# Linear attention and a gated feed-forward layer: keys of the third batch in the first chunk, two accumulators in turn, and turned queries and rows loaded at once

## The chip, the cores and the metric

The kernel runs on one core of a Trainium2 chip. The core has five engines that run side by side, each with its own queue of instructions: TensorE (PE in the profile; its weight loads are PEld), VectorE (DVE), ScalarE (ACT), GpSimd (POOL) and SyncE (SP), which here issues all DMA transfers. The metric is the time of one execution on the device in microseconds; several timed runs are given with their median. A profile is one further execution, recorded instruction by instruction.

## The reference

There are 8 batches with 8 heads, 576 tokens a batch and 64 elements a head. Linear attention is followed by a gated feed-forward layer over all 4608 tokens:

```python
q_s = exp(q - max(q, axis=-1));  q_s = q_s / (sum(q_s, axis=-1) + 1e-9)   # per token and head
k_s = exp(k - max(k, axis=2));   k_s = k_s / (sum(k_s, axis=2) + 1e-9)    # over a batch's tokens
kv  = einsum('bhsd,bhse->bhde', k_s, v)                                   # 64 x 64 per head
x   = einsum('bhsd,bhde->bhse', q_s, kv)       # -> x of 4608 x 512
out = ((x @ w_a) * (x @ w_b)) @ w_out          # 512 -> 1536 -> 512
```

All inputs are float32.

## The kernel before

**Chunks.** The 4608 tokens are worked in nine chunks of 512 tokens. Each chunk needs `x` of its own tokens (attention) and then runs the feed-forward layer over them. Two heads make a group (`g`, four of them), so that a group fills 128 partitions. A batch has 576 tokens and a chunk 512, so a chunk needs the `kv` matrices of one or two batches. float32 products are made as three products of a high and a low part (`split`, L76: ScalarE or VectorE writes the high part, VectorE the low part as a difference).

**The first chunk** (L636 to L651) goes over 12 blocks `f` of the inner dimension. Each step loads the weights of a later block, converts them from the 64-bit form in which they arrive (`to_float`, L87: ScalarE, VectorE, GpSimd, VectorE), writes parts of them back to DRAM, multiplies (`gate_first`, L419) and projects the block before (`project_first`, L457). Beside this runs the attention of the second chunk.

**The chunks after it** (L666 to L729) make the gated products with seven block products instead of eight (`product`, L443), for six steps `i` of two blocks. The seven weight operands of a step come from DRAM (`get_w`, L163, eight buffers `ws`), or, in the second chunk, are partly formed from sums by GpSimd (`sums`, L168) and then split. The seven operands that stand for `x` are formed by `x_operands` (L392) from the tile `xf`, which the attention fills.

**Attention beside the products.** `attention_tasks(c)` (L490) returns a list of steps for chunk `c`, and each step is a list of functions. `Spread` (L571) hands these steps out, so many at each call: `attend()` once for each `f` from 1 in the first chunk, `attend(last)` three times for each `i` later. In the later chunks, VectorE's instructions of a call are queued behind the VectorE instruction `last` (`issue_after`); those of other engines aren't. Apart from that a planner orders each engine's instructions: it takes those that are ready by its own estimates, earlier ones of the program first. It also gives out buffers: tiles with one tag share a number of buffers (`bufs`), and a new tile waits until an older one of that tag has been read for the last time. PSUM has eight banks here, under the tags `at`, `k0`, `k1`, `k2` and `po0` to `po3`.

**Keys.** For each batch and group: load keys and values (`k_load`, `v_load`, two buffers each), maximum over the tokens, subtract, exponential (`kv_soft`, L198), product with the values (`kv_product`, L248), and split (`kv_split`, L267). For the third batch (`b == 2`) the maximum over the partitions goes over PE: a transpose `pm`, a reduction and a diagonal matrix on VectorE, and a product `pmx` (L206 to L216); for later batches it is one instruction of GpSimd. The loop of L494 adds a batch's keys to the tasks of the first chunk that needs it; for the third batch that is chunk 2, whose attention runs beside the products of chunk 1, the second chunk.

**Queries.** For the second chunk (`c < LATE`, which is 2) a group's queries are normalised as rows, turned by PE (`q_transpose`, L361: `pq`), split, and multiplied with `kv` (`x_product`, L372: `px`); ScalarE copies the result to `xf` (L532). Both `pq` and `px` have the tag `at`. For the chunks from the third on, rows give the statistics alone (`q_stats`, L317); these are turned and written to DRAM as `dq` (`q_stats_out`, L330). The queries are then read a second time in turned form from the input `qt_late` (tile `qtt`, tag `kt`, two buffers), and the statistics come back as rows repeated over 64 partitions (tile `mr`, two buffers; `q_turned`, L341). `q_exp` (L353) adds the negative maximum, takes the exponential and splits; after `px` VectorE multiplies by the reciprocal of the sum (L562). The three parts `b0` (loads), `b1` (`q_exp`) and `b2` (product) of the four groups are pipelined: in one step `b0` of a group, `b1` of the one before, `b2` of the one before that.

Of the kernel before, what the change touches and what calls it, by code (L numbers as in the profile page):

```python
# [29 lines left out]
def linear_attention_then_gated_ffn(  # L30
# [299 lines left out]
    def q_stats_out(c, st):  # L330

        n = NP * 2 * 2 * TT
        pst = ps.tile([n, P], F32, name="pst", tag="at")
        nc.tensor.transpose(pst, st.rearrange("p g h w j -> p (g h w j)"), ident)
        sst = sb.tile([n, P], F32, name="sst", bufs=1)
        nc.vector.tensor_copy(out=sst, in_=pst)
        dq = dr.tile([n, P], F32, name=f"dq{c}")
        nc.sync.dma_start(out=dq, in_=sst)
        return dq.rearrange("(g h wj) p -> g h (wj p)", g=NP, h=2)

    def q_turned(c, g, dq):  # L341

        qt = sb.tile([P, T], F32, name="qtt", tag="kt")
        nc.sync.dma_start(out=qt, in_=qt_late[c - LATE, g])
        mr = sb.tile([P, 2, T], F32, name="mr", bufs=2)
        for h in range(2):
            nc.sync.dma_start(
                out=mr[h * D:(h + 1) * D].rearrange("d w t -> d (w t)"),
                in_=dq[g, h].unsqueeze(0).broadcast_to([D, 2 * T]),
            )  # L350
        return qt, mr

    def q_exp(qt, mr):  # L353
        nc.vector.tensor_tensor(out=qt, in0=qt, in1=mr[:, 0], op=ALU.add)  # L354
        nc.scalar.activation(out=qt, in_=qt, func=AF.Exp)  # L355
        qh = sb.tile([P, T], F32R, name="qh", bufs=1)
        ql = sb.tile([P, T], F32R, name="ql", bufs=1)
        split(qh, ql, qt)
        return qh, ql
# [130 lines left out]
    def attention_tasks(c):  # L490

        xfs[c] = sb.tile([P, NP, T], F32, name="xf", bufs=1)
        steps = []
        for b in range(c * T // S, (c * T + T - 1) // S + 1):  # L494
            if b in batch_done:
                continue
            batch_done.add(b)
            for g in range(NP):
                box = {}

                def s0(b=b, g=g, box=box):
                    box["t"] = ((k_load_t if b == 1 else k_load)(b, g), v_load(b, g))

                def s1(b=b, box=box):
                    kt = box["t"][0]
                    box["e"] = kv_soft_t(kt, ("k2", "at")) if b == 1 else kv_soft(b, kt)

                def s2(b=b, g=g, box=box):
                    kv_split(b, g, kv_product(box["e"], box["t"][1]))

                steps.append((s0, s1, s2))
        def pipeline(steps):

            parts = max((len(p) for p in steps), default=0)
            return [
                [steps[i - j][j] for j in range(parts) if 0 <= i - j < len(steps)]
                for i in range(len(steps) + parts - 1)
            ]

        if c < LATE:  # L520
            for g in range(NP):
# [8 lines left out]
                def s2(c=c, g=g, box=box):  # L530
                    px = x_product(c, g, q_transpose(box["e"]))
# [4 lines left out]
        stats, last = [], []  # L536
        every = {}
        for g in range(NP):
# [15 lines left out]
            def b0(g=g, box=box):  # L554
                box["q"] = q_turned(c, g, every["dq"])

            def b1(box=box):
                box["e"] = q_exp(*box["q"])

            def b2(g=g, box=box):  # L560
                px = x_product(c, g, box["e"])
                nc.vector.tensor_tensor(out=xfs[c][:, g], in0=px, in1=box["q"][1][:, 1], op=ALU.mult)  # L562

            last.append((b0, b1, b2))
        stats, steps = pipeline(stats), pipeline(steps)
        seq = []
        for i in range(max(len(stats), len(steps))):
            seq.append((stats[i] if i < len(stats) else []) + (steps[i] if i < len(steps) else []))
        return seq + pipeline(last)
# [66 lines left out]
    for f in range(NF):  # L636
# [5 lines left out]
        if f:  # L642
            attend()
        if f == NF - 1:
# [138 lines left out]
```

## Time and profile before

| | |
|---|---|
| timed runs | 990.72, 988.35, 991.26 us; median 990.72 us |
| profiled execution | 984.57 us, its span 982.6 us |
| granted clock of TensorE, mean | 0.991 |
| DMA | 283.64 MB |

The page gives times in microseconds and calls engines by the short names above. "L449" is line 449 of the kernel before. In rows of groups stand, after the line, engine and operation, what is written and read ("out<-in"), the shape, the count ("x48"), then the busy time, the mean duration of one in ns, and the idle time of the engine just before them with what ended it. "PE px L381 <- DVE ql L82: 1.8, 3, 1.2" means that PE at L381 stood idle until VectorE's L82 was done, 1.8 us in all, three times, at most 1.2 us. In rows of a timeline stand start, duration, engine, line and operation, and in brackets the idle time before. PE's matmuls overlap, so their durations in a row add up to more than the time they take in sequence. In rows of windows the number in brackets is the count of instructions; the columns are named where the rows are shown.

### The profile page before, as it was taken

To read this page: it belongs to the slowest core of one execution; us is meant where nothing else is said; L and a number is where in the kernel's file an instruction comes from. 1 tells how busy PE (TensorE), PEld (TensorE's weight loads), DVE (VectorE), ACT (ScalarE), POOL (GpSimd) and SP (SyncE) were. 2 spreads that over 40 slices of the span, in tenths; PEclk is the share of its full clock that TensorE was granted. 3 is DMA by queue.
4 is the path that set the end of the run, shared out by engine and by line. 5 is a ranking of instruction groups with operands and counts; after the bars stand their busy time and mean duration, and the time that the engine had idled before them with its cause. 6 is when DMAs were issued, how large, how long until landed. Compare 5 with 4: busy or idle time off the path is not lost.

```text
span 982.6 us, 16989 instructions
## 1 busy us (share of the span) xinstructions
PE 948.5 (97%) x6171; PEld 851.9 (87%) x6171; DVE 629.2 (64%) x1257; ACT 391.4 (40%) x1085; POOL 112.8 (11%) x96
## 2 busy tenths in 40 slices
PE   4889999999999999999999999999999999999998
PEld 3657666899999999989999999999999999899997
DVE  7797786887685656656576557655666546653433
ACT  8665675632273325322442235223532263221101
POOL 3245345441000000000000000000000000000000
PEclk9799999999999999999999999999999999999999
DMA  9699858999989968997799779977998689767761
GB/s 347 222 412 402 343 207 294 373 327 305 301 285 352 320 237 280 325 328 250 248 335 324 271 251 345 319 270 257 331 299 299 220 300 283 274 224 271 246 207 61
DMA packets 93682, 283.64 MB, mean 289 GB/s; under 512 B 10848, under 2 KB 11424, under 8 KB 93600
## 3 DMA queue, kind: packets, MB, share of 16 engines
q1 hardware_dynamic: 93600, 282.57, 82.3%
q8 instruction: 49, 0.80, 0.3%
q14 instruction: 33, 0.27, 0.1%
HBM read 241.40 MB, written 37.98 MB: 284 GB/s over the span
## 4 chain that ended last, share of the span: by engine, by line
PE 78%; DMA 8%; DVE 5%; issue 4%; POOL 2%; ACT 2%; SPq 0%; POOLq 0%; DVEq 0%; ACTq 0%
PE po L470 25%; PE kp L449 13%; PE kx L449 13%; PE ka L449 12%; PE ky L449 6%; PE pk L251 3%; PE px L381 2%; POOL wr L103 2%; DMA mr<-dq 2%; PE po L459 2%; PE pt L426 2%; DMA qtt<-in_q_late 1%; DMA wo_raw<-in_w_out 1%; DMA dw<-ws 1%; DVE ws L82 1%
## 5 line engine op out<-in xcount | busy, mean ns | idle before, releaser
L470 PE MATMUL po<-wo_w,gh 128*128 128x512 f32 x768 | 227.2, 394 | 0.0
L449 PE MATMUL kx<-xo,ws 128*128 128x256 f32 x1152 | 164.5, 284 | 0.0
L449 PE MATMUL ka<-xo,ws 128*128 128x256 f32 x1152 | 162.3, 284 | 0.2
L470 PEld LDWEIGHTS po<-wo_w,gh 128*128 128x128 f32 x768 | 138.9, 189 | 26.2 <-ACT gh L79 0.3
L449 PE MATMUL kp<-xo,ws 128*128 128x256 f32 x1152 | 158.3, 284 | 0.8 <-DVE cc L712 0.8
L449 PEld LDWEIGHTS ka<-xo,ws 128*128 128x128 f32 x1152 | 151.2, 191 | 4.0 <-ACT xo L79 0.3
L449 PEld LDWEIGHTS kx<-xo,ws 128*128 128x128 f32 x1152 | 151.6, 191 | 3.4 <-issue 0.5
L449 PEld LDWEIGHTS kp<-xo,ws 128*128 128x128 f32 x1152 | 148.2, 191 | 3.6 <-DVE cc L712 1.0
L470 PE MATMUL po<-wo_w,gl 128*128 128x512 f32 x384 | 137.7, 396 | 0.0
L79 ACT CAST gh<-cc 128x512 fp32r<-128x512 f32 x96 | 57.7, 620 | 148.5 <-DVE cc L723 145.1
L722 DVE TENSOR_TENSOR cc<-kp,u 128x512 f32<-128x512 f32 x48 | 33.0, 688 | 89.2 <-PE kp L449 89.0
L323 ACT ACTIVATE qt<-qt,st 128x64 f32<-128x64 f32 x224 | 75.0, 337 | 31.7 <-DVE st L320 27.8
L470 PEld LDWEIGHTS po<-wo_w,gl 128*128 128x128 f32 x384 | 71.2, 188 | 15.8 <-DVE gl L82 0.4
L449 PE MATMUL ky<-xo,ws 128*128 128x256 f32 x576 | 79.4, 287 | 2.5 <-ACT xo L79 2.1
L426 PE MATMUL pt<-xo,ws 128*128 128x512 f32 x288 | 74.1, 406 | 4.0 <-ACT ga L433 3.2
L449 PEld LDWEIGHTS ky<-xo,ws 128*128 128x128 f32 x576 | 73.8, 194 | 3.2 <-ACT xo L79 2.4
L82 DVE TENSOR_TENSOR gl<-cc,gh 128x512 fp32r<-128x512 f32 x96 | 66.8, 703 | 9.4 <-ACT gh L79 9.2
L426 PEld LDWEIGHTS pt<-xo,ws 128*128 128x128 f32 x288 | 53.3, 188 | 20.4 <-ACT ga L433 4.7
L713 ACT COPY cc<-kx 128x256 f32<-128x256 f32 x48 | 17.8, 371 | 128.3 <-PE kx L449 120.6
L219 POOL PARTITION_ALL_REDUCE mx<-m x20 | 14.1, 704 | 470.9 <-DVE m L205 438.1
L712 DVE TENSOR_TENSOR cc<-kp,u 128x512 f32<-128x512 f32 x48 | 32.9, 684 | 52.3 <-PE kp L449 52.2
L355 ACT ACTIVATE qtt<-qtt 128x512 f32<-128x512 f32 x28 | 17.7, 633 | 107.4 <-DVE qtt L354 81.5
(126 smaller groups left out, 1238.7 us busy)
## 6 DMA issues: line engine op xcount, KB each, us to landing
ws<-dw SPq DMA_DIRECT2D x312, 512.0 KB, 5.3
dw<-ws SPq DMA_DIRECT2D x42, 512.0 KB, 4.9
mr<-dq SPq DMA_DIRECT2D x56, 256.0 KB, 6.3
raw<-in_w_ab SPq DMA_DIRECT2D x24, 512.0 KB, 8.1
out<-ot SPq DMA_DIRECT2D x36, 256.0 KB, 4.5
vt<-in_v SPq DMA_DIRECT2D x28, 325.0 KB, 7.5
qt<-in_q SPq DMA_DIRECT2D x32, 256.0 KB, 5.3
kt<-in_k SPq DMA_DIRECT2D x24, 320.0 KB, 6.0
```

What stands on the lines that cost most here:

```text
L79: nc.scalar.copy(out=hi, in_=src)
L82: nc.vector.tensor_tensor(out=lo, in0=src, in1=hi.bitcast(F32), op=ALU.subtract)
L103: nc.gpsimd.tensor_tensor(out=r, in0=u, in1=r, op=ALU.add)
L251: nc.tensor.matmul(pk, kt[:, j].rearrange("p h d -> p (h d)"), vt[:, j], start=(j == 0), stop=(j == J - 1),)
L323: nc.scalar.activation(out=qt[:, j, h], in_=qt[:, j, h], func=AF.Exp, bias=st[:, h, 0, j:j + 1], accum_out=st[:, h, 1, j:j + 1],)
L381: nc.tensor.matmul(px[:, s], w, m[:, s], start=(i == 0), stop=(i == 2))
L426: nc.tensor.matmul(pt, w[:, wp], x[g][:, xp], start=(i == 0), stop=(i == 3 * NP - 1))
L449: ins = nc.tensor.matmul(pt[:, n], w[:, n, wp, c], x[:, xp, c], start=(first and n == 0 and i == 0), stop=(i == 5), skip_group_check=True,)
L459: nc.tensor.matmul(po[t], g[:, t * P:(t + 1) * P], wo[f][:, 1].bitcast(F32), start=(f == 0), stop=(f == NF - 1),)
L470: ins = nc.tensor.matmul(po[t], a[:, ts], wo[f][:, w], start=(f == 0 and i == 0), stop=(f == NF - 1 and i == 2),)
L712: nc.vector.tensor_tensor(out=cc[:, 3], in0=kp, in1=u3, op=ALU.add)
L722: nc.vector.tensor_tensor(out=cc[:, 1], in0=kp, in1=u2, op=ALU.add)
```

## The change

Three things are changed.

- The loop that adds keys becomes a function `key_steps(batches, tag)`. In the first chunk, from `f == 8` on, the keys of the third batch are handed out over the last four steps by a `Spread` of their own, behind `attend()`. Chunk 2's tasks then hold no keys. VectorE's instructions of these steps are not queued behind `last`.
- For the second chunk's queries `pq` and `px` take the tag `at` for even groups and `k2` for odd groups.
- For chunks after the third (`roomy(c)`, so `c > 2`) the four turned queries have buffers of their own (`qh`, `ql` and the two of `kt`), the rows are eight tiles under the tag `wy` (whose eight buffers held converted weights in the first two chunks), and the split queries take the two buffers of `mr`. Loads are no part of the pipeline any more: two steps behind the statistics hold the loads of groups 0 and 1, then of 2 and 3; after them comes the pipeline of `b1` and `b2` alone. In all chunks from the third on each row DMA is halved: it brings the maximum or the reciprocal sum of one head (64 partitions of 2 KB) where it brought both.

```diff
@@ -336,25 +336,45 @@
         nc.vector.tensor_copy(out=sst, in_=pst)
         dq = dr.tile([n, P], F32, name=f"dq{c}")
         nc.sync.dma_start(out=dq, in_=sst)
-        return dq.rearrange("(g h wj) p -> g h (wj p)", g=NP, h=2)
-
-    def q_turned(c, g, dq):
-
-        qt = sb.tile([P, T], F32, name="qtt", tag="kt")
+        return dq.rearrange("(g h w j) p -> g h w (j p)", g=NP, h=2, w=2)
+
+
+
+    def roomy(c):
+        return c > LATE
+
+    def q_turned(c, g):
+        if roomy(c):
+            tag, bufs = (("qh", 1), ("ql", 1), ("kt", None), ("kt", None))[g]
+        else:
+            tag, bufs = "kt", None
+        qt = sb.tile([P, T], F32, name="qtt", tag=tag, bufs=bufs)
         nc.sync.dma_start(out=qt, in_=qt_late[c - LATE, g])
-        mr = sb.tile([P, 2, T], F32, name="mr", bufs=2)
+        return qt
+
+    def q_rows(c, g, dq):
+
+        if roomy(c):
+            rows = [sb.tile([P, T], F32, name=f"mr{w}", tag="wy", bufs=8) for w in range(2)]
+        else:
+            mr = sb.tile([P, 2, T], F32, name="mr", bufs=2)
+            rows = [mr[:, w] for w in range(2)]
         for h in range(2):
-            nc.sync.dma_start(
-                out=mr[h * D:(h + 1) * D].rearrange("d w t -> d (w t)"),
-                in_=dq[g, h].unsqueeze(0).broadcast_to([D, 2 * T]),
-            )
-        return qt, mr
-
-    def q_exp(qt, mr):
-        nc.vector.tensor_tensor(out=qt, in0=qt, in1=mr[:, 0], op=ALU.add)
+            for w in range(2):
+                nc.sync.dma_start(
+                    out=rows[w][h * D:(h + 1) * D], in_=dq[g, h, w].unsqueeze(0).broadcast_to([D, T])
+                )
+        return rows
+
+    def q_exp(c, qt, rows):
+        nc.vector.tensor_tensor(out=qt, in0=qt, in1=rows[0], op=ALU.add)
         nc.scalar.activation(out=qt, in_=qt, func=AF.Exp)
-        qh = sb.tile([P, T], F32R, name="qh", bufs=1)
-        ql = sb.tile([P, T], F32R, name="ql", bufs=1)
+        if roomy(c):
+            hl = sb.tile([P, 2, T], F32R, name="qhl", tag="mr", bufs=2)
+            qh, ql = hl[:, 0], hl[:, 1]
+        else:
+            qh = sb.tile([P, T], F32R, name="qh", bufs=1)
+            ql = sb.tile([P, T], F32R, name="ql", bufs=1)
         split(qh, ql, qt)
         return qh, ql
 
@@ -487,11 +507,18 @@
     batch_done = set()
     xfs = {}
 
-    def attention_tasks(c):
-
-        xfs[c] = sb.tile([P, NP, T], F32, name="xf", bufs=1)
+    def pipeline(steps):
+
+        parts = max((len(p) for p in steps), default=0)
+        return [
+            [steps[i - j][j] for j in range(parts) if 0 <= i - j < len(steps)]
+            for i in range(len(steps) + parts - 1)
+        ]
+
+    def key_steps(batches, tag="at"):
+
         steps = []
-        for b in range(c * T // S, (c * T + T - 1) // S + 1):
+        for b in batches:
             if b in batch_done:
                 continue
             batch_done.add(b)
@@ -503,20 +530,21 @@
 
                 def s1(b=b, box=box):
                     kt = box["t"][0]
-                    box["e"] = kv_soft_t(kt, ("k2", "at")) if b == 1 else kv_soft(b, kt)
+                    if b == 1:
+                        box["e"] = kv_soft_t(kt, ("k2", "at"))
+                    else:
+                        box["e"] = kv_soft(b, kt, (tag, tag))
 
                 def s2(b=b, g=g, box=box):
-                    kv_split(b, g, kv_product(box["e"], box["t"][1]))
+                    kv_split(b, g, kv_product(box["e"], box["t"][1], tag))
 
                 steps.append((s0, s1, s2))
-        def pipeline(steps):
-
-            parts = max((len(p) for p in steps), default=0)
-            return [
-                [steps[i - j][j] for j in range(parts) if 0 <= i - j < len(steps)]
-                for i in range(len(steps) + parts - 1)
-            ]
-
+        return steps
+
+    def attention_tasks(c):
+
+        xfs[c] = sb.tile([P, NP, T], F32, name="xf", bufs=1)
+        steps = key_steps(range(c * T // S, (c * T + T - 1) // S + 1))
         if c < LATE:
             for g in range(NP):
                 box = {}
@@ -528,12 +556,14 @@
                     box["e"] = (q_soft_first if c == 1 else q_soft)(box["q"])
 
                 def s2(c=c, g=g, box=box):
-                    px = x_product(c, g, q_transpose(box["e"]))
+
+                    tag = ("at", "k2")[g % 2] if c == 1 else "at"
+                    px = x_product(c, g, q_transpose(box["e"], tag), tag)
                     nc.scalar.copy(out=xfs[c][:, g], in_=px)
 
                 steps.append((s0, s1, s2))
             return pipeline(steps)
-        stats, last = [], []
+        stats, last, turned, rows = [], [], [], []
         every = {}
         for g in range(NP):
             box = {}
@@ -551,21 +581,29 @@
             stats.append((a0, a1))
             box = {}
 
-            def b0(g=g, box=box):
-                box["q"] = q_turned(c, g, every["dq"])
+            def t0(g=g, box=box):
+                box["q"] = q_turned(c, g)
+
+            def r0(g=g, box=box):
+                box["r"] = q_rows(c, g, every["dq"])
 
             def b1(box=box):
-                box["e"] = q_exp(*box["q"])
+                box["e"] = q_exp(c, box["q"], box["r"])
 
             def b2(g=g, box=box):
                 px = x_product(c, g, box["e"])
-                nc.vector.tensor_tensor(out=xfs[c][:, g], in0=px, in1=box["q"][1][:, 1], op=ALU.mult)
-
-            last.append((b0, b1, b2))
+                nc.vector.tensor_tensor(out=xfs[c][:, g], in0=px, in1=box["r"][1], op=ALU.mult)
+
+            turned.append(t0)
+            rows.append(r0)
+            last.append((b1, b2) if roomy(c) else (lambda t0=t0, r0=r0: (t0(), r0()), b1, b2))
         stats, steps = pipeline(stats), pipeline(steps)
         seq = []
         for i in range(max(len(stats), len(steps))):
             seq.append((stats[i] if i < len(stats) else []) + (steps[i] if i < len(steps) else []))
+        if roomy(c):
+
+            seq += [rows[:2] + turned[:2], rows[2:] + turned[2:]]
         return seq + pipeline(last)
 
     class Spread:
@@ -641,6 +679,10 @@
             convert_f(f + 2)
         if f:
             attend()
+        if f == 8:
+            keys = Spread(pipeline(key_steps((2,), "at")), 4)
+        if f >= 8:
+            keys()
         if f == NF - 1:
             sy[0] = sums(0)
             x_operands(xfs[1], early + late, xo)
```

## The prediction

> **What bounds the kernel now.** I read the page first, then the waits of PE by window, then the timelines of the places where it waits. The page's head, busy row and DMA row:
>
> ```profile
> span 982.6 us, 16989 instructions
> PE 948.5 (97%) x6171; PEld 851.9 (87%) x6171; DVE 629.2 (64%) x1257; ACT 391.4 (40%) x1085; POOL 112.8 (11%) x96
> DMA packets 93682, 283.64 MB, mean 289 GB/s; under 512 B 10848, under 2 KB 11424, under 8 KB 93600
> ```
>
> PE is busy for 948.5 of 982.6 us, and the change takes no matmul away: it moves some, and gives others a different bank. So no more can be won than PE's idle time, plus the stretches in which PE runs slowly. The question is which idle time the three edits reach. They reach two places. The first is the passage from the first chunk to the second and what follows it; the second is the attention of the later chunks. PE's waits in these two windows (160 to 216 us, then 300 to 900 us; columns: total, times, longest):
>
> ```profile
> PE ky L449 <- ACT xo L79: 2.1, 1, 2.1
> PE pm L210 <- DVE kt L222: 1.2, 1, 1.2
> PE pm L210 <- DVE m L205: 0.7, 1, 0.7
> PE ky L449 <- DVE cc L722: 0.5, 1, 0.5
> ...
> PE px L381 <- DVE ql L82: 1.8, 3, 1.2
> PE kp L449 <- DVE cc L712: 0.8, 1, 0.8
> PE px L381 <- ACT qh L79: 0.3, 1, 0.3
> ```
>
> The first window has 4.5 us, the second 2.9 us. The first wait also has an after-effect. The same passage by single microseconds (columns: PE busy with its matmuls, PEld, DVE, ACT, POOL, granted clock, DMA share, GB/s):
>
> ```profile
> 167.00:168.00 1.00, 0.34 (x1) 0.29 (x1) 0.92 (x2) 1.00 (x2) 0.00 (x0) 0.79 1.06 426
> 168.00:169.00 1.00, 0.98 (x4) 0.74 (x4) 1.00 (x3) 1.00 (x3) 0.00 (x0) 0.50 1.04 393
> 169.00:170.00 1.00, 1.00 (x7) 1.00 (x6) 1.00 (x2) 1.00 (x3) 0.00 (x0) 0.50 1.03 393
> 170.00:171.00 1.00, 1.00 (x7) 1.00 (x7) 1.00 (x3) 0.29 (x1) 0.00 (x0) 0.50 1.04 401
> 171.00:172.00 1.00, 1.00 (x10) 1.00 (x10) 1.00 (x3) 0.62 (x1) 0.99 (x1) 1.00 0.95 381
> ```
>
> After the wait the granted clock is 0.50 for about 3.4 us (0.4 of the first row and the next three). Half speed for 3.4 us is 1.7 us of work lost. So the passage costs 2.1 + 1.7 = 3.8 us. The Trainium skill (TensorE: Matmul & The Clock Gate, Part 1: The HAM clock gate) has the clock fall after at least one idle window of about 3.4 us; by that rule a wait of 2.1 us would leave the clock alone and the passage would be worth 2.1 us only. Here the trace shows 0.50 behind the short wait, and the measurement decides.
>
> **The change part by part.**
>
> **A. Two banks in turn for the second chunk's queries.** Per group of queries a transpose writes `pq`, it is split, the product `px` is made and copied to `xf`. All of it goes through the bank "at", so group 3 cannot start its transpose before group 2 is copied out. POOL's last scaling of the queries, and PE at the end of the chunk:
>
> ```profile
> 146.84 1.04 POOL L293 TENSOR_TENSOR qt<-qt,qst 128x512 f32<-128x512 f32 x1 [1.70 <-PE pq L364]
> ```
>
> ```profile
> 159.87 0.60 PE L364 MATMUL pq<-ident,qt 128*128 128x128 f32 x4
> ...
> 164.40 0.30 PE L381 MATMUL px<-qh,kvh 128*128 128x64 f32 x1
> ...
> 167.66 0.58 PE L449 MATMUL ky<-xo,ws 128*128 128x256 f32 x1 [2.05 <-ACT xo L79]
> ```
>
> The queries of group 3 are ready at 147.9 us, but their transpose runs at 159.87 and their product at 164.40, as the last thing before PE runs dry at 165.6. What follows is serial: copy `xf`, difference `xt`, split `xo`, and `ky` at 167.66. With its own bank ("k2" for odd groups) the transpose no longer has to wait for group 2, so the product can come up to 12 us (159.9 less 147.9) earlier, and 3 us earlier suffices to hide the 2.1 us chain under the output products, which then come last. The number of instructions is unchanged, nothing is queued behind a new wait, and "k2" is otherwise idle there (its next user is the second chunk's `ka`). Gain between 0 and 3.8 us. I take 3.0, near the upper end, because the serial chain stands in the rows above; the remainder is left for the planner, which still chooses the order.
>
> **B. The third batch's keys go to the last four steps of the first chunk.** This moves four groups, each a load of keys and values, maximum, two small PE steps with VectorE between them, exponential, five products and a split. What they cost now, in 168 to 262 us (busy us, mean ns):
>
> ```profile
> L251 PE MATMUL pk<-vt,kt 128*128 128x130 f32 x40 | 5.1, 274 | 0.0
> ...
> L222 DVE TENSOR_TENSOR kt<-kt,pmx 128x640 f32<-128x640 f32 x4 | 3.3, 814 | 3.7 <-PE pmx L216 3.7
> ...
> L204 DVE TENSOR_TENSOR m<-m 128x128 f32<-128x128 f32 x4 | 2.2, 554 | 0.0
> L203 DVE TENSOR_TENSOR m<-kt 128x256 f32<-128x256 f32 x4 | 2.1, 534 | 0.0
> ...
> L216 PE MATMUL pmx<-m,ones 128*128 128x128 f32 x8 | 1.6, 278 | 0.0
> L81 DVE CAST kvh<-kv 128x128 fp32r<-128x128 f32 x4 | 1.4, 349 | 0.1
> ...
> L210 PE MATMUL pm<-ident,m 128*128 128x128 f32 x4 | 1.2, 300 | 2.0 <-DVE kt L222 1.2 <-DVE m L205 0.7
> ...
> L256 DVE TENSOR_SCALAR den<-pk 128x1 f32<-128x1 f32 x4 | 0.6, 155 | 1.4 <-PE pk L251 1.3
> ```
>
> VectorE: 3.3 + 2.2 + 2.1 + 1.4 + 0.6, and seven more groups of the list between 0.6 and 1.4 us, some 7 us: about 16 us. PE: up to 5.1 + 1.6 + 1.2 = 7.9 us, which is moved and not saved, since PE is full at both places. Where it goes (columns as above):
>
> ```profile
> 120.00:130.00 10.00, 9.78 (x40) 6.87 (x39) 6.71 (x12) 6.67 (x12) 3.83 (x3) 1.00 0.44 157
> 130.00:140.00 10.00, 10.00 (x34) 5.86 (x34) 9.65 (x14) 6.88 (x18) 4.33 (x5) 1.00 0.49 190
> 140.00:150.00 10.00, 10.00 (x41) 6.95 (x39) 7.91 (x14) 7.52 (x32) 3.88 (x3) 1.00 0.84 275
> 150.00:160.00 10.00, 10.00 (x44) 7.20 (x43) 4.20 (x5) 3.46 (x6) 8.72 (x7) 1.00 0.56 212
> 160.00:170.00 10.00, 7.93 (x34) 5.20 (x33) 9.20 (x12) 7.53 (x14) 2.52 (x2) 0.88 0.97 348
> ```
>
> VectorE has 50 less 37.7, or 12.3 us idle there, and the chunk grows by the moved PE work, some 7 us: 19 us of room for 16 us. It fits, narrowly. The DMA share is 0.44 to 0.56 in three of these five rows, and part of the loads runs there already: SP's first key load of this batch is issued at 100.50, before this chunk ends.
>
> ```profile
> 100.50 0.33 SPq L189 DMA_DIRECT2D kt<-in_k  x1
> ```
>
> What is removed from the second chunk are the two waits of `pm` (1.2 and 0.7) and the wait of `ky` for `cc` (0.5), in which VectorE worked on this batch: 2.4 us. The two small PE steps can wait for VectorE in the new place too, and there the conversions, the splits and the chunk's other work on VectorE and PE queue behind them. The same kind of wait moved at its full size gives 0; twice its size (VectorE is at 9.65 of 10 in one row) loses 2.4. I take a gain of 1.5, nearer to the removed rows, because in four of the five rows VectorE has more air than it has in the second chunk.
>
> **C. Rows and turned queries of the later chunks.** Now each group's turned queries need one of two "kt" buffers and its rows one of two "mr" buffers, so the loads of group 2 wait until group 0 is consumed. VectorE's and SP's waits in 300 to 960 and 300 to 900 us:
>
> ```profile
> DVE qtt L354 <- DMA mr<-dq: 29.3, 14, 4.5
> DVE qtt L354 <- DMA qtt<-in_q_late: 12.6, 4, 3.4
> ```
>
> ```profile
> SPq L347 <- DVE xf L562: 28.9, 10, 4.1
> ```
>
> SP waits for the consumer, then VectorE waits for the load, and PE for VectorE: the three waits of 1.8 + 0.8 + 0.3 = 2.9 us. Afterwards eight row tiles and four query tiles exist at once, so neither wait remains; what is late next is the plain chain of VectorE and ScalarE work, which also gets two split buffers instead of one. The attention list becomes one step longer (13 for 12, of 15 calls), still before the next chunk's operands. I take 2.5 of 2.9.
>
> What it adds: the rows are loaded in four pieces of 128 KB per group instead of two of 256 KB, so eight more issues on SP per chunk, and they come in two bursts.
>
> ```profile
> 310.00 2.37 SPq L347 DMA_DIRECT2D mr<-dq  x4
> ```
>
> At 2.37 / 4 = 0.6 us an issue, a burst of eight rows and two query tiles holds SP for about 6 us, and 1.5 MB at the page's mean of 289 GB/s holds the queue for about 5 us. Behind it stand the weight loads (the issue row, then the same place of two successive steps in the chain in order of time):
>
> ```profile
> ws<-dw SPq DMA_DIRECT2D x312, 512.0 KB, 5.3
> ```
>
> ```profile
> 899.03 2.80 PE po L470 x12
> ...
> 914.66 2.80 PE po L470 x12
> ```
>
> A step lasts 15.6 us and uses 7 of the 8 weight tiles, so a tile comes round every 8/7 of that, 17.9 us; less 5.3 us for the load, some 12 us remain, less the product itself (1.4) about 11. One burst of 6 us is covered; two back to back (12 us) just aren't. No wait of PE for a weight load stands in the list now. Cost taken: 0; ends: 0, and 2 us in each of six chunks.
>
> **Sum.** 3.0 + 1.5 + 2.5 = 7.0 us. The profiled execution took 984.57 us (span 982.6 and 2.0 around it), which becomes 977.6. The three timed runs have a median of 990.72, 6.2 us longer than the profiled one; I take the gain off that: 983.7 us.
>
> **The rivals.**
>
> 1. *VectorE is the next bound at the passage.* The 16 us do not fit in time, because groups 2 and 3 of the keys wait for their two buffers, and the second chunk's operands queue behind them. For it: 9.65 and 9.20 of 10 busy in two of the rows. Against: 5.8 us of idle VectorE in 150 to 160 alone. A and B give 0, C stays: 988.2.
> 2. *The later waits stay*, because the DMA engines rather than the buffers set when rows land, or PE is ordered otherwise and waits elsewhere. For it: VectorE's 29.3 us of waiting for rows. Against: SP's 28.9 us for the consumer. A and B stay: 986.2.
> 3. *All goes*, with the small losses of clock and pipeline around each wait. Upper ends 3.8 + 2.4 + 2.9 = 9.1, and as much as a further 2 us: 980.
> 4. *Slower: the bursts make the weight loads late.* Place: the chunks from the third on, right after the statistics come back. It decides when SP or the queue holds the weight loads for over 11 us, thus when both bursts come back to back. Price: 2 us a chunk, six chunks, 12 us, less A and B of 4.5: 7.5 us slower, 998.2. For it: 12 us of issuing stands against 11. Against: the two bursts are one call (5 us) apart, and the loads that are needed first were issued before.
>
> That the batch is not moved at all in effect (the planner runs its VectorE work only when that engine has nothing earlier to do) gives the numbers of rival 1.
>
> **How the numbers follow.** Forecast 0.40, rival 1 0.20, rival 2 0.14, rival 3 0.16, rival 4 0.10. About 0.3%, or 3 us, can be told from no change here: faster means under 987.7. Forecast, rival 2 and rival 3 lie there, 0.70; rival 1 lies within, and with part of the edges 0.19; slower keeps 0.11. The range takes rival 3 and rival 1 in, with B's lost 2.4 us on top of 988.2: 978.5 to 991; outside lie rival 4 and a few in a hundred below.
>
> **What would show it.** A: the last `px` of the first chunk lies before the last `po` products, `ky` has no wait for `xo`, and the clock stays at 1.00 near 170 us. B: `pm` and `pmx` stand before the passage with waits under 1 us, and none after. C: no `px` wait for `ql` after 300 us; SP no longer waits for `xf`. Wrong would be: a wait of PE for a weight load, a second row at 0.50, or waits of `pm` in the first chunk that exceed 2.4 us.

## The result and the profile after

| | before | after |
|---|---|---|
| median beside each other (5 runs each) | 988.35 us | 977.28 us |
| lowest and highest | 987.0, 991.26 | 976.46, 978.01 |
| profiled execution, and its span | 984.57, 982.6 | 977.28, 975.2 |

The ratio is 0.988, with a 95% interval of 0.9864 to 0.9896: the change is 11 us faster. The forecast was 7.0 us off a median of 990.72, thus 983.7 with a range from 978.5; the time lies 1.2 us below the range. Between the two profiled executions the difference is 7.3 us, almost the sum; but that agreement is a coincidence, as the runs below show.

The page of the changed kernel, its span, busy row and DMA row, and the chain by engine:

```profile
span 975.2 us, 17022 instructions
PE 946.0 (97%) x6171; PEld 851.7 (87%) x6171; DVE 633.9 (65%) x1257; ACT 391.7 (40%) x1085; POOL 114.3 (12%) x96
DMA packets 98162, 283.65 MB, mean 291 GB/s; under 512 B 11744, under 2 KB 12320, under 8 KB 98080
PE 89%; DVE 5%; ACT 2%; DMA 2%; issue 1%; SPq 0%; DVEq 0%; ACTq 0%
```

The last of these rows in the kernel before:

```profile
PE 78%; DMA 8%; DVE 5%; issue 4%; POOL 2%; ACT 2%; SPq 0%; POOLq 0%; DVEq 0%; ACTq 0%
```

The matmuls are as many as before, PE's share of the chain rises from 78% to 89%, and DMA's falls from 8% to 2%. PE's waits in the two windows of the prediction (160 to 216 us, then 300 to 900 us):

```profile
PE pmx L216 <- DVE m L214: 0.8, 1, 0.8
PE ka L469 <- issue: 0.6, 1, 0.6
PE po L490 <- ACT gh L79: 0.6, 1, 0.6
PE ky L469 <- DVE cc L764: 0.2, 1, 0.2
...
PE ky L469 <- DMA ws<-dw: 0.4, 1, 0.4
```

The first window has 2.2 us where it had 4.5, the second 0.4 where it had 2.9. The last products of the first chunk, in PE's timeline, and the passage by microseconds (PE, PEld, DVE, ACT, POOL, granted clock, DMA share, GB/s):

```profile
161.75 0.19 PE L401 MATMUL px<-qh,kvh 128*128 128x64 f32 x1
...
164.95 2.74 PE L479 MATMUL po<-wo_w,ga 128*128 128x512 f32 x6
167.13 0.68 PE L469 MATMUL ky<-xo,ws 128*128 128x256 f32 x1
```

```profile
167.00:168.00 1.00, 1.00 (x7) 0.66 (x6) 1.00 (x2) 1.00 (x3) 0.00 (x0) 1.00 1.37 256
168.00:169.00 1.00, 1.00 (x11) 1.00 (x10) 1.00 (x3) 1.00 (x3) 0.00 (x0) 1.00 0.69 178
```

Step A is seen as forecast: the last query product stands ahead of the last output products, `ky` waits for nothing, and the clock stays at 1.00. Step C is seen too: no wait of `px` is left after 300 us, SP no longer waits for `xf`, and VectorE's wait for rows, 29.3 us before, is down to one (300 to 960 us):

```profile
DVE qtt L370 <- DMA mr<-dq: 3.1, 1, 3.1
```

Step B is seen only in half. The transposes `pm` of the four key groups, one each:

```profile
L210 PE MATMUL pm<-ident,m x4: 271/271/272, 125.8 to 204.1; 128*128 128x128 f32 x4
```

They lie at 125.8, 160.5, 183.3 and 204.1 us: two groups ahead of the passage, two still behind it. The two waits of `pm` (1.2 and 0.7 us) are gone, but at 184 us `pmx` now waits 0.8 us for VectorE.

Two of the signs that were to show the forecast wrong stand in this profile too: the wait of PE for a weight load (0.4 us), and a stretch at clock 0.50, near 73 us instead of 168. The last section comes back to that stretch.

### The profile page after: what moved, and what is told of

Its sections match the earlier page's. It is cut to its first block, busy times and chain, and to the rows that moved or that the text cites. A ratio compares the mean times of both kernels' runs of the same rounds, so it can differ in the third digit from the quotient of the medians.

```text
span 975.2 us, 17022 instructions
## 1 busy us (share of the span) xinstructions
PE 946.0 (97%) x6171; PEld 851.7 (87%) x6171; DVE 633.9 (65%) x1257; ACT 391.7 (40%) x1085; POOL 114.3 (12%) x96
## 4 chain that ended last, share of the span: by engine, by line
PE 89%; DVE 5%; ACT 2%; DMA 2%; issue 1%; SPq 0%; DVEq 0%; ACTq 0%
PE po L490 27%; PE kp L469 14%; PE ka L469 14%; PE kx L469 14%; PE ky L469 7%; PE pt L446 5%; PE pk L251 3%; PE po L479 3%; PE px L401 3%; DVE ws L82 1%; DVE wy L104 1%; DMA ws<-dw 1%; DMA kt_first<-in_kt 1%; DMA dw<-ws 0%; ACT qt L323 0%
## 5 line engine op out<-in xcount | busy, mean ns | idle before, releaser
L490 PE MATMUL po<-wo_w,gh 128*128 128x512 f32 x768 | 229.5, 394 | 0.6 <-ACT gh L79 0.6
L490 PE MATMUL po<-wo_w,gl 128*128 128x512 f32 x384 | 140.1, 396 | 0.0
L740 ACT COPY u<-kx 128x512 f32<-128x512 f32 x48 | 28.0, 583 | 83.6 <-PE kx L469 81.4
```

What stands on the lines that cost most here:

```text
L490: ins = nc.tensor.matmul(po[t], a[:, ts], wo[f][:, w], start=(f == 0 and i == 0), stop=(f == NF - 1 and i == 2),)
L740: nc.scalar.copy(out=u2, in_=kx)
```

## The experiments

All medians stand beside runs of the kernel before on the same chip, whose median moved between 988.4 and 991.0 us. Three kernels have one edit each, two have two edits.

**The kernel before, again.**

> The kernel before, unchanged, to see what its own executions differ by. Theory 1 (the profiled execution of before was a lucky one: its wait near 70 us was not followed by a stretch at half clock, others of its executions have one or more such stretches): this profile shows a different set of stretches at clock 0.50 than the one at hand (there one, near 168 us), and the time follows their number at about 1.7 us each; median 986 to 990. Theory 2 (the 3.8 us between the profiled execution and the median is a chip or a day that is slower everywhere): the same set of stretches, and the time is longer by a like share in all windows.

Median 989.2 us, 12 runs from 984.48 to 995.12; ratio 1.0015 (0.9991 to 1.0039). The profiled execution of before, 984.57 us, is thus at the fast end of its own spread. This run's profile is of an execution of 994.08 us. Its PE waits from 300 to 960 us, and three microseconds of it:

```profile
PE px L381 <- ACT qh L79: 4.4, 3, 3.1
PE px L381 <- DVE ql L82: 1.9, 4, 0.8
PE kp L449 <- DVE cc L712: 0.4, 1, 0.4
```

```profile
345.00:346.00 1.00, 0.00 (x0) 0.00 (x0) 1.00 (x3) 0.70 (x2) 0.00 (x0) 0.70 1.06 430
346.00:347.00 1.00, 0.40 (x2) 0.40 (x3) 1.00 (x3) 0.55 (x1) 0.00 (x0) 0.50 0.97 385
347.00:348.00 1.00, 1.00 (x6) 1.00 (x6) 1.00 (x4) 0.59 (x2) 0.00 (x0) 0.50 0.69 279
```

The same program, the same order on each engine: the later waits are 6.7 us instead of 2.9, and one of them, 3.1 us long, is followed by half clock. Theory 1 is right in kind (another set of stretches at 0.50), but the waits themselves vary as well. The passage shows it too: `ky` waits 2.05 us for `xo` as in the profile before, but this time the clock stays at 1.00 behind it:

```profile
170.00:171.00 1.00, 1.00 (x10) 1.00 (x10) 1.00 (x3) 1.00 (x3) 0.00 (x0) 1.00 0.95 352
```

**C alone.** The edit is `roomy`, all that asks for it, and the halved row DMAs; the two other edits are left out:

```diff
-        if f == 8:
-            keys = Spread(pipeline(key_steps((2,), "at")), 4)
-        if f >= 8:
-            keys()
...
-                    tag = ("at", "k2")[g % 2] if c == 1 else "at"
+                    tag = "at"
```

(against the changed kernel).

> Edit C alone: from the fourth chunk on turned queries and rows loaded at once, the rest as before. Theory: the waits of px for ql after 300 us go, 2.5 us (2.9 by the listed waits; some 4 to 5 if the short losses around each wait go too). Rival (the bursts make weight loads late): waits of PE for ws, 0 or slower.

982.89 us, ratio 0.9937 (0.9914 to 0.9959): 6 us faster, against 2.5 forecast. Its six runs lie between 981.31 and 984.0. After 300 us one wait is left:

```profile
PE kx L469 <- DMA ws<-dw: 0.2, 1, 0.2
```

The profiles of all kernels here show where the 6 us lie. From PE's first `ky` of the fourth chunk to the end, the six executions without C take 608.7 to 617.0 us (608.7, 609.8, 611.0, 612.2, 615.1, 617.0), and the fourteen with C take 605.0 to 606.5. PE's listed waits from 300 to 900 us are 1.3 to 6.8 us in the six, and 0 to 1.7 us in the fourteen. Four of the six have stretches of half clock between 320 and 870 us, none of the fourteen has one between 300 and 970 us.

**A alone.**

```diff
-                    px = x_product(c, g, q_transpose(box["e"]))
+                    tag = ("at", "k2")[g % 2] if c == 1 else "at"
+                    px = x_product(c, g, q_transpose(box["e"], tag), tag)
```

> Edit A alone: the second chunk's queries take the two banks in turn, keys and rows as before. Theory (the serial chain through one bank made PE run dry at the passage): no wait of ky for xo, no half clock near 168 us, the time falls by 3.0 us (0 to 3.8 by the prediction). Rival (VectorE is the next bound at the passage and the operands stay late): under 1 us.

992.18 us, ratio 1.0028 (1.0009 to 1.0047): nothing won, rather some 3 us lost. The mechanism works (`px` of the last group at 161.13 us, `ky` at 165.93 without a wait), but other waits stand behind it, from 160 to 345 us:

```profile
PE ky L449 <- ACT xo L79: 2.2, 1, 2.2
PE kp L449 <- DVE cc L713: 2.1, 1, 2.1
PE ka L449 <- issue: 1.7, 1, 1.7
```

The wait of `ky` is back, but at 278 us, at the passage from the second chunk to the third. That these waits make up the 3 us is not shown, since without C the waits after 300 us (here that of `kp`) differ between executions anyway.

**B alone.**

```diff
+        if f == 8:
+            keys = Spread(pipeline(key_steps((2,), "at")), 4)
+        if f >= 8:
+            keys()
```

> Edit B alone: the third batch's keys over the last four steps of the first chunk, one bank for the queries, rows as before. Theory: 1.5 us from the removed waits of pm in the second chunk, the passage stays dry. Rival 1 (the moved work fills PE's dry passage with useful matmuls, which neither the forecast nor the rivals counted): the wait for xo shrinks or goes although the bank is shared, and 3 to 6 us are won. Rival 2 (the same waits moved): 0 or slower.

1006.34 us, ratio 1.0174 (1.0149 to 1.02): 17 us slower. PE's timeline, SP's issue of the key load that it waits for, VectorE's first use of it, and clock and engines in two stretches:

```profile
178.10 0.45 PE L210 MATMUL pm<-ident,m 128*128 128x128 f32 x1 [8.14 <-DVE m L205]
184.55 1.09 PE L384 MATMUL pq<-ident,qt 128*128 128x128 f32 x4 [1.04 <-DVE kvh L81]
188.00 0.42 PE L401 MATMUL px<-qh,kvh 128*128 128x64 f32 x1 [2.36 <-DVE ql L82]
```

```profile
170.45 0.55 SPq L189 DMA_DIRECT2D kt<-in_k  x1
```

```profile
176.88 0.42 DVE L203 TENSOR_TENSOR m<-kt 128x256 f32<-128x256 f32 x1 [3.94 <-DMA kt<-in_k]
```

```profile
174.00:178.00 4.00, 0.00 (x0) 0.00 (x0) 1.01 (x3) 0.00 (x0) 1.40 (x2) 0.50 0.75 294
178.00:184.00 6.00, 3.74 (x13) 2.92 (x13) 1.78 (x6) 0.74 (x1) 0.00 (x0) 0.50 0.00 0
```

The last queries stand behind two key groups in the one bank; the key group waits for one of two buffers and then 6.4 us for its load. The product that the second chunk needs comes at 188 us, PE is idle for 8 us, and the clock stays at half from 173 to 197 us (23.9 us, which by half of it is some 12 us of work lost).

**B alone with another bank for the keys.**

```diff
-            keys = Spread(pipeline(key_steps((2,), "at")), 4)
+            keys = Spread(pipeline(key_steps((2,), "k2")), 4)
```

> Edit B alone, but the third batch's keys use the bank k2 and the queries stay in at. Theory (the shared bank makes B alone slow): the 8 us wait of pm that ends the first chunk and the half clock behind it go, the time falls by 12 us or more against B alone, to before or below. Rival (VectorE's and the loads' work in the first chunk makes B alone slow): 10 us or more slower than before remain.

1003.74 us, ratio 1.0127 (1.0096 to 1.0159). The wait of 8 us goes, yet 13 us remain, so the shared bank is only part of it. PE's longest waits from 160 to 220 us are now split up, over the operands among others:

```profile
PE pm L210 <- DVE m L205: 2.5, 2, 2.0
PE ky L469 <- DVE xo L82: 2.3, 1, 2.3
...
PE ky L469 <- ACT xo L79: 1.1, 1, 1.1
```

The last query product (167.8 us) stays late without A, and VectorE then has keys and operands at once. This fits rival 1 of the prediction, which gave it no price beyond the lost gain.

**A and B, without C.**

> Edits A and B together, rows as before (the change less C). Theory (B alone put the last queries of the second chunk behind two groups of keys in the one bank at, and A gives them a bank of their own): none of the 17 us of B alone remains, the passage is not dry, 4 to 6 us faster than before, and the later waits of px stay as in before. Rival (A and B are worth nothing together either, and the whole gain is C's 6.2): within 1.5 us of before.

984.08 us, ratio 0.9935 (0.9913 to 0.9958): 6.5 us faster, where A alone costs 3 and B alone 17. The waits of `px` after 300 us stay (4.6 and 2.2 us in its profile).

**A and C, without B**, and the same once more:

> Edits A and C together, keys of the third batch in the second chunk as before (the change less B). Theory (A and B need each other: with the keys' VectorE work behind the passage A alone won nothing): 6 to 7 us faster than before, which is C alone, and 4 to 5 us slower than the whole change. Rival (A does its work once C has taken the noise away, B is worthless): as fast as the whole change, 10 to 11 us.

> Edits A and C without B once more, on the same chip, to compare the run beside it with: 981 to 982.5 us, 8 to 9 us faster than before, with the wait of ky for xo near 275 us.

981.59 us, ratio 0.9914 (0.9896 to 0.9932), and 981.55, ratio 0.9918 (0.9893 to 0.9944): 9.1 and 7.0 us faster than the kernel before beside them, and 4.5 us slower than all three on the same chip (977.06 us, below). So A no longer costs anything beside C, and B is worth some 4.5 us. The dry passage near 275 us is there both times; this is the first of the two:

```profile
274.99 0.39 PE L469 MATMUL ky<-xo,ws 128*128 128x256 f32 x1 [2.16 <-ACT xo L79]
```

**The change again.**

> The whole change again, on the chip of these runs. Theory 1 (C takes away waits that differ from execution to execution): its runs lie within 2 us of each other, those of before within 8 to 12 us; 10 to 12 us faster than before. Theory 2 (the chip's own spread): both spread alike.

977.06 us (976.24 to 977.97), ratio 0.9865 (0.9845 to 0.9885). Its six runs differ by 1.7 us, the eleven of before beside them by 6.6. C takes away the spread of the later chunks (605.0 to 606.5 us where it was 608.7 to 617.0), not all of it: the second six runs of A and C differ by 6.9 us.

**What of C does it.** The loads stay in the pipeline, with the change's buffers:

```diff
-            last.append((b1, b2) if roomy(c) else (lambda t0=t0, r0=r0: (t0(), r0()), b1, b2))
+            last.append((lambda t0=t0, r0=r0: (t0(), r0()), b1, b2))
...
-        if roomy(c):
-            seq += [rows[:2] + turned[:2], rows[2:] + turned[2:]]
```

> The whole change, but the loads of the later chunks stay in the pipeline, one group a step, with the buffers of the change (rows, turned queries and split queries apart). Theory (C's gain comes from the buffers: no load waits for a consumer any more): within 1.5 us of the whole change, 11 to 13 us faster than before, no waits of px for ql after 300 us. Rival (it comes from the lead of the loads, all at once and earlier): 3 to 6 us slower than the whole change, with waits of px again.

976.7 us, ratio 0.9866 (0.9838 to 0.9895): as fast as the change. So it does not matter that all is loaded at once; the buffers are what is left of C, together with the halved row loads, from which no kernel here separates them in these chunks. The burst that rival 4 feared exists in the change: SP's row issues in the third chunk,

```profile
306.33 12.30 SPq L364 DMA_DIRECT2D mr<-dq  x16
```

all sixteen issues in 12.3 us, the two bursts back to back (in the five chunks after it 10.2 to 12.0 us). That is more than the 11 us at which the rival decides, but PE's only wait for a weight load after 300 us is the 0.4 us shown above, at 624.9 us, behind the burst of 606 to 617 us.

**More of the keys ahead.** Steps from `f == 6` over six calls; the third group's keys and values in the two `mr` buffers; both.

```diff
-        if f == 8:
-            keys = Spread(pipeline(key_steps((2,), "at")), 4)
-        if f >= 8:
+        if f == 6:
+            keys = Spread(pipeline(key_steps((2,), "at")), 6)
+        if f >= 6:
```

```diff
+                    kt = vt = None
+                    if b == 2 and g == 2:
+                        kt = sb.tile([P, J, 2, D], F32, name="kt", tag="mr", bufs=2)
+                        vt = sb.tile([P, J, 2, D + 1], F32, name="vt", tag="mr", bufs=2)
-                    box["t"] = ((k_load_t if b == 1 else k_load)(b, g), v_load(b, g))
+                    box["t"] = ((k_load_t if b == 1 else k_load)(b, g, kt), v_load(b, g, vt))
```

> The whole change with the third batch's keys handed out from f = 6 over six steps. Theory (the keys' place is set by when their VectorE work gets a turn): all four groups move ahead, waits of pm after the passage go, 1 to 2 us faster than the whole change. Rival (the two buffers of keys and values, busy with the second batch before, set it): same as the whole change.

> The whole change, with keys and values of the third batch's third group loaded into the two buffers that the rows use later. Theory (two key buffers leave half of the batch behind the passage): pm of group 3 comes before 167 us, three groups in the first chunk, the wait of pmx at 183 us goes; 0.5 to 2 us faster than the whole change. Rival (VectorE is full at the passage, more keys there make the operands late, as in B alone): a wait of ky for xo and a stretch at half clock, 3 us or more slower.

> The whole change with both of the last two: from f = 6, and the third group in buffers of its own. Theory: all four groups ahead of the passage, 1 to 3 us faster than the whole change. Rival (VectorE full at the passage): slower by 3 us or more, with a wait of ky for xo.

981.67 us (0.9916, 0.989 to 0.9941), 980.77 (0.9904, 0.9877 to 0.993) and 983.89 (0.9942, 0.9923 to 0.9961): all slower than the kernel just shown on the same chip (976.7 us), which is as fast as the change. With steps from `f == 6` three `pm` come ahead of the passage (the third at 166.66 us); the last query product comes late and waits for VectorE, and the clock falls behind it. That the keys now stand ahead of the queries in the bank fits this, but was not tried by itself:

```profile
168.41 0.30 PE L401 MATMUL px<-qh,kvh 128*128 128x64 f32 x1 [1.44 <-DVE ql L82]
```

```profile
170.00:174.00 4.00, 2.77 (x12) 2.48 (x12) 4.00 (x4) 2.28 (x5) 3.84 (x3) 0.55 0.99 390
```

VectorE is busy for all of these 4 us. In the change itself it is at 9.96 and 10.00 of 10 in the two rows at the passage:

```profile
160.00:170.00 10.00, 10.00 (x55) 7.18 (x54) 9.96 (x16) 6.51 (x13) 2.59 (x2) 1.00 1.02 337
170.00:180.00 10.00, 9.35 (x76) 8.88 (x74) 10.00 (x19) 3.91 (x12) 6.81 (x4) 1.00 1.03 402
```

So there is no room for more there. The second kernel didn't move what it was made to move: its third `pm` comes at 180.5 us, behind the passage, and it loses elsewhere, above all at 117 us, where PE waits and half clock follows:

```profile
PE px L401 <- DVE ql L82: 1.7, 1, 1.7
```

It tells nothing of the buffers. With both edits, three `pm` are ahead again and the losses at the passage return.

**Where B's 4.5 us come from.** Four kernels end the third chunk's tasks earlier or free one of its buffers: its list over fewer calls (without B, and in the change), its turned queries in free buffers of the operands (without B, and with the loads in the pipeline and B).

```diff
-        attend = Spread(attention_tasks(c + 1) if more else [], 3 * NI - 3 - (1 if c == 1 else 0))
+        attend = Spread(attention_tasks(c + 1) if more else [], 11 if c == 1 else 3 * NI - 3)
```

```diff
-            tag, bufs = "kt", None
+            tag, bufs = "xo", 11
```

> Edits A and C without B, as before in the keys' place, but the third chunk's tasks are handed out over 11 calls instead of 14, so that their 12 steps end one call earlier, where the 11 steps of the whole change end. Theory (what B wins is not at the keys' old place but that the third chunk's last product no longer comes right before the passage from the second chunk to the third): no wait of ky for xo near 275 us, 3 to 4.5 us faster than A and C alone, within 1.5 us of the whole change. Rival (B wins by the moved VectorE work itself): as A and C alone, 981 to 982 us.

> The whole change, with the third chunk's tasks over 10 calls instead of 14, one call earlier once more. Theory (the second passage is already covered in the whole change, where only short waits of 0.7 to 0.9 us stand): within 1 us of the whole change. Rival (an earlier end wins again): 1 to 2 us faster.

> Edits A and C without B, and the third chunk's turned queries in four free buffers of the operands instead of the two of the keys. Theory (the third chunk's turned queries queue behind the third batch's keys for two buffers, so its products end right before the passage to the third chunk, and B wins by emptying these buffers earlier): the first turned query is loaded before 225 us instead of 239, the wait of ky for xo near 275 us goes, 2.5 to 4.5 us faster than A and C alone. Rival (the chain is paced by something else, such as VectorE or the row buffers): within 1 us of A and C alone, the wait stays.

> The whole change with the loads in the pipeline (as run once already: 976.7 us) and the third chunk's turned queries in the free buffers of the operands. Theory (little is left at that passage, waits under 1 us): 0 to 1.5 us faster than that. Rival (every reordering there makes a new dry passage, as ending the list earlier did): 4 us or more slower.

984.5 (0.9949, 0.9923 to 0.9976), 984.32 (0.994, 0.9917 to 0.9963), 985.09 (0.9945, 0.9924 to 0.9966) and 986.3 us (0.9965, 0.9947 to 0.9983). The two with B (the second and the fourth) are clearly slower than the same kernel without the edit; the two without B are slower than A and C by the medians, with intervals that overlap. All four have the wait of 2.2 us of `ky` near 275 to 280 us. All four theories fell. What the traces have in common is the third chunk's rows. SP's issues of the rows of groups 2 and 3, without B (A and C), then in the repetition of the change:

```profile
255.50 2.37 SPq L364 DMA_DIRECT2D mr<-dq  x4
...
261.90 2.38 SPq L364 DMA_DIRECT2D mr<-dq  x4
```

```profile
249.66 2.37 SPq L364 DMA_DIRECT2D mr<-dq  x4
...
255.13 2.57 SPq L364 DMA_DIRECT2D mr<-dq  x4
```

For two row buffers, each of these issues comes only after an earlier group's product has been scaled into `xf`; in A and C SP waits for that, from 200 to 276 us:

```profile
SPq L364 <- DVE xf L595: 5.7, 2, 4.0
```

The last kernel gives the rows buffers of their own, without B:

```diff
-            mr = sb.tile([P, 2, T], F32, name="mr", bufs=2)
+            mr = sb.tile([P, 2, T], F32, name="mr", tag="xo", bufs=11)
```

> Edits A and C without B, and the third chunk's rows in four free buffers of the operands instead of two of their own. Theory (in all runs so far the passage to the third chunk is dry where the third chunk's last rows are issued less than 15 us before it, and is not where they are issued 17 us or more before; the rows wait for a buffer that a product of an earlier group must free): the last rows are issued before 255 us instead of 262, the wait of ky near 275 us goes, 2.5 to 4.5 us faster than A and C alone (981.6 us). Rival (the rows follow the chain and don't lead it): the wait stays, within 1 us of A and C alone or slower.

SP's last row issue for that chunk, and PE's waits from 260 to 300 us:

```profile
240.25 3.51 SPq L364 DMA_DIRECT2D mr<-dq  x4
```

```profile
PE po L490 <- ACT gh L79: 0.7, 1, 0.7
PE px L401 <- ACT qh L79: 0.3, 1, 0.3
```

The rows are issued by 244 us and the wait of `ky` is gone. 979.75 us, ratio 0.9911 (0.9887 to 0.9935). Against the 981.6 of its two partners (on other chips) this is 1.8 us by the medians, less than the 2.5 expected; by the ratios (0.9914 and 0.9918) it is under 1 us, and the intervals overlap. Without B the dry passage is thus shown to hang on the row buffers; what its end is worth is not shown. The profiles, of one execution each, point to a gain: PE reaches the fourth chunk at 374.5 and 372.4 us in A and C, at 370.9 here, and at 369.5 and 370.4 in the change. One difference to the change that stays is seen: near 173 us `ka` waits 1.4 to 1.7 us for ScalarE's split of the weights in both profiles of A and C and here, 0.6 us in the change. By the medians most of B's share, some 2.7 us, stays unexplained.

## Why the prediction was right and wrong

**The direction and the places were right.** PE's waits at the passage and after 300 us are what went, and A and C work by the mechanisms that were named: the last query product comes 2.7 us earlier than before (161.75 for 164.40, where 3 were said to suffice), and the loads wait for no consumer.

**The step that failed is the term of C, "I take 2.5 of 2.9".** C alone measured 6 us. The gain was 11.1 us where 7.0 were forecast, and these 3.5 us are most of the 4.1 that are missing. (The base moved too: the three runs that the forecast started from have a median of 990.72 us, the five beside the result 988.35; the time lies only 1.2 us below the range, so that either of the two is enough to put it there.) The term was read from the wait list of one execution. That execution was near the fastest of its kernel (984.57 us, where runs go from 984.5 to 997.0). In the next one these waits were 6.7 us, with half clock behind one, and over six profiles without C they are 1.3 to 6.8 us. What the runs show in its place: from the fourth chunk on the kernels take 608.7 to 617.0 us without C and 605.0 to 606.5 with it. The hint was on the table: the prediction saw that the profiled execution was 6.2 us under the median, carried that difference over to the changed kernel as if it were a constant, and did not ask which waits make it. A large part of it are those that C removes; the changed kernel's profiled execution is at its median.

**B's reason was wrong.** "The two waits of pm ... 2.4 us; I take 1.5": two of four groups still run in the second chunk, and a wait of `pmx` of 0.8 us is still there. "It fits, narrowly" was wrong too: VectorE is full at the passage with half of the keys moved, and the two kernels that get a third group ahead are slower. Alone, the move costs 17 us, more than any rival allowed (the worst was 7.5 us); the load that waits for one of two key buffers was named there, but not that the last queries would stand behind it in the bank.

**The sum itself was wrong as a sum.** It added A, B and C. Measured: A costs 3 us, B costs 17, together they win 6.5. A frees the passage, and PE then meets the next late chain (the third chunk's, 110 us later); B, which needs A's bank, makes that chain earlier (its last rows are issued at 255 us instead of 262). With C the three win 11.1 us here and 13.7 in the repetition. That the forecast for A and B together, 4.5 us, is near what they win on top of C (11.1 less 5.8, thus 5.3 us) is luck: neither term was right by itself.

**The clock's share was right in kind.** The passage cost 2.1 us of waiting and 1.7 of half clock in the profile before, and both are gone. But the 1.7 us were chance: in the second profile of the kernel before the same wait has no half clock behind it. One stretch of half clock near 73 us is in the changed kernel's profile and not in that of before. The 7.3 us between the two profiles hold several such chances; that they are near the forecast of 7.0 proves nothing. In these two profiles PE even reaches the third chunk at the same time (273.7 us), and all of the difference lies behind that.

**The rivals.** Rival 3 has the measured gain (9.1 and up to 2 more, thus up to 11.1 us), but not by its terms: it too adds 2.9 us for C, and 2.4 for B. Rival 4 had its cause right (12.3 us of issuing, over the 11 that it asks for) and not its effect, 0.4 us of waiting once. Why the weights came in time all the same is not shown; the prediction's own argument against this rival, that the loads that are needed first were issued before, fits.

## What to carry to other kernels

Waits behind loads can differ from execution to execution (here 2.9 and 6.7 us in two of one program): before a term is read from them, compare the profiled execution with the spread of the timed ones, and where it lies at the fast end, expect more than the listed waits. Buffers that let a load run ahead of its consumer can then win more than one trace shows. Edits that touch the same bank, buffers or engine at one passage are to be costed together: what one wins, the next late chain takes, until another edit moves that too.

## What was not expected of the hardware

The clock falls after short waits, and not always. Near 71 us PE waits 2.1 to 2.2 us in 18 of the 20 profiles, at a place that no edit here is meant to change. In the changed kernel's profile the clock is at half behind it, in the profile of its repetition it isn't:

```profile
73.00:74.00 1.00, 1.00 (x4) 0.71 (x4) 0.52 (x1) 1.00 (x3) 0.00 (x0) 0.50 1.08 426
74.00:75.00 1.00, 1.00 (x4) 0.81 (x3) 0.48 (x2) 0.48 (x1) 0.00 (x0) 0.50 1.00 401
```

```profile
73.00:74.00 1.00, 1.00 (x6) 0.79 (x5) 0.44 (x1) 1.00 (x3) 0.00 (x0) 1.00 1.07 420
74.00:75.00 1.00, 1.00 (x7) 0.78 (x6) 0.59 (x2) 0.37 (x1) 0.09 (x1) 1.00 1.03 416
```

Of the 18 profiles with this wait, nine have the half clock, for 3.4 us each, so one and the same wait costs 2.2 or 3.9 us. The traces show where the difference lies. Within each of the 20 executions the clock falls and rises on one grid of 3.41 us (in the profile of before, the stretches at 0.50 begin at 20.81, 34.47 and 167.59 us: 4 and 39 times 3.413 us apart), and only the place of the grid differs from execution to execution. In the nine profiles with half clock, 2.12 us or more of the wait near 71 us lie in one interval of the grid; in the other nine a boundary divides the wait, and the larger piece is 1.09 to 1.75 us. At the passage it is the same: 1.98 us in one interval in the profile before, and half clock; 1.08 and 0.98 us in its second profile, and none. A threshold doesn't follow from this: near 275 us pieces of 1.4 and 1.9 us were followed by half clock too. The Trainium skill (TensorE: Matmul & The Clock Gate, Part 1: The HAM clock gate) says that the window over which activity is judged runs freely and doesn't start with the kernel; the grid seen here agrees with that, while its idle time of about 3.4 us before the clock falls is longer than the 2.1 to 2.2 us that suffice here.
